# One place in the order of issue for each of 2222 operations, instead of a periodic table of places

## The chip, the cores and the metric

The kernel runs on one core of a Trainium2 chip. The metric is the device time of one execution in microseconds (us). In the profile PE is TensorE's matmul, PEld its weight load, DVE is VectorE, ACT is ScalarE, POOL is GpSimd and SP is SyncE, which here issues DMAs only. An instruction of an engine waits at the head of that engine's queue until what it needs is there, and everything behind it in the same queue waits with it.

## What is computed

Two state-space convolutions (S4D) of the same input, mixed by a gate. The input `u` has 2048 positions and 512 channels; each of the two branches has its own parameters and 128 states for each channel.

```python
def branch(u, log_A_real, A_imag, C_real, C_imag, log_dt, D_skip):
    dt = exp(log_dt)
    A = -exp(log_A_real) + 1j * A_imag
    C = (C_real + 1j * C_imag) * dt[:, None]
    P = exp((A * dt[:, None])[:, :, None] * arange(L))      # channel, state, position
    K = 2.0 * einsum("dn,dnl->dl", C, P).real               # the filter of each channel
    y = irfft(rfft(u.T, 2 * L) * rfft(K, 2 * L))[..., :L]   # causal convolution
    return y.T + u * D_skip
g = sigmoid((u * gate_w).sum(-1, keepdims=True))
out = g * branch_A(u) + (1 - g) * branch_B(u)
```

## The kernel before

All work is float32, apart from the phases, whose angles are carried as three bfloat16 terms. There are 1024 filters (512 channels, two branches). They are worked on in three nested sizes:

- A **chunk** `c` (8 of them) is 128 filters. Its preparation, `prep_ops(c)`, is a list of 34 steps on `[128, 128]` tiles: angles and amplitudes on DVE and ACT (L175 to L198, L256), a split of the angles into three bfloat16 terms (`split`, L216, and `rest`, L221), a bounce of these through device memory by SP (`bounce`, L225, then `back`, L231 and L233, which writes the tile `rot`), and the decay rates by PE and ACT (`turned`, L242 to L244, `dec`, L248). Then `make_bases` (L301) makes 28 exponentials on ACT in seven parts of four, and `amplitudes` (L305) finishes them on DVE.
- A **unit** `u` (64 of them, eight for a chunk) is 16 filters. It has fifteen operations: `phase` on PE (L335, reads `rot`), `sine` (L343), `absf` (L346) and `cosine` (L350) on ACT, two grids (L355) and four products (L371, L383, L389, L393) on DVE, `modes` on PE (64 small matmuls, L401), `keep` on ACT (L408), `skip` on DVE (L413), `s1_k` on PE (L419) and `keep_x` on ACT (L426), which writes a part of the tile `xall`.
- A **block** `b` (16 of them) is four units. Its operations multiply the spectra of the filters with that of the input: `s2` on PE (L463), `products` on DVE (L476), eight of each; four DMAs by POOL, `add_products` (L510), which add one half of the products onto the other half within `xall`; four `inverse` on PE (L521) that wait for these DMAs; four `keep_z` on ACT (L527). The input's own spectrum comes from `s1_u` on PE (L439) and `keep_u` on ACT (L447), and for every second block `keep_v`, `turn_v`, `negate_v` and `both_v` (L487 to L503) lay it out in the tile `v` with ACT and SP's DMAs.

At the end of each quarter of the channels `final` (L548, PE), `final_keep` (L557, ACT) and `final_out` (L560, SP) make the output; the last quarter has a form of its own (L569 to L594). A gate (L602 to L620) is made once near the start. Sin, Exp and Sigmoid need different tables on ACT, which the compiler loads before an ACTIVATE that needs another table than the last one (ACT_TABLE_LOAD in the profile).

What sets the order: every operation is put into a list with a number, its key, and the list is issued in the order of the keys. While it is issued, each instruction of PE, DVE and ACT is tied to the instruction before it on its engine, so the three engines run exactly in this order. A key is a home plus an offset from the table `AT`. One unit is 1.0 of key. The offsets are periodic: a unit's operations have four offsets (by `u % 4`), a block's have one set for even and one for odd blocks, a chunk's 34 steps have one set for all chunks but the first two:

```python
    def op(name, home, fn, i=None, *args):
        at = AT[name] if i is None else AT[name][i]
        ops.append((home + at, len(ops), name, fn, args, (name, i), home))
```

The home of unit `u` is `u`, of chunk `c` it is `8 * (c - 1)`, of block `b` it is `4 * (b + 1)`. So the offset 5.5876 of the last `split` of a chunk and the offset -1.3428 of a chunk's first `phase` place these two 8 - 1.3428 - 5.5876 = 1.07 units apart, in each chunk from the third on. The loops at the end of the function (`for c in range(nchunk)` and those after it) only fill the list. Bounds that the order meets: `rot` has two buffers (by `c % 2`), the tiles of a unit (`f0`, `f1`, `fsn`) two each, `ph`, `pk`, `ps1` and `ks` one each, and the PSUM tiles of `s2`, `s1_u`, `inverse` and `turned` share three.

Of the kernel before, what the change touches and what calls it, by code (L numbers as in the profile page):

```python
# [10 lines left out]
F32 = mybir.dt.float32  # L11
# [29 lines left out]

# [4 lines left out]
def tile_gated_s4d(ctx: ExitStack, tc: tile.TileContext, nsb, a, out):  # L46
    nc = tc.nc
# [57 lines left out]
    for i, (o, x) in enumerate(consts):  # L105
        op("ld", 0, lambda o=o, x=x: nc.sync.dma_start(out=o, in_=x), i)
# [432 lines left out]
    def final(sb, j, dp, r4):  # L539
# [5 lines left out]
        for n in range(2):  # L545
            for rq in range(4):
# [16 lines left out]
    ends_e = []  # L563

    def last_e(g):
        if g % 2 == 0:
            tag = "fsn" if g < 4 else "f0"
            ends_e.append(work.tile([128, 2, 8, 2, 64], F32, name="el", tag=tag, bufs=BUFS[tag]))
            nc.gpsimd.memset(ends_e[-1], 0.0)  # L569
# [64 lines left out]
    d0, p0 = make_dt(), prep_ops(0)  # L634
    for n, fn in enumerate(first + d0 + p0):
        op("first", 0, fn, n)
    for c in range(nchunk):
        h = 8 * (c - 1)
        if c > 0:
            e = AT["early"] if c == 1 else 0  # L640
            op("pl", h if c > 1 else -1, load_pars, None, c)
            op("al", h if c > 1 else -1, decay_rate, None, c)
            for i, fn in enumerate(prep_ops(c)):
                op("prep", h - e, fn, i)
        for i in range(7):
            op("ex", h if c else h + 0.2, make_bases, i, c, i)
        op("ba", h if c else h + 0.2, amplitudes, None, c)
    for u in range(nunit):
        for name, fn in (
            ("ph", phase), ("sn", sine), ("ab", absf),  # L650
            ("cs", cosine), ("g1", grid1), ("g0", grid0), ("p1", prod1), ("pm", prod_minus),
            ("pc", prod_cos), ("pn", prod_sin), ("mo", modes), ("ke", keep), ("kd", skip), ("s1", s1_k), ("xk", keep_x),
        ):
            op(name, u + AT["start"].get((u, name), 0) + AT["stop"].get((nunit - u, name), 0), fn, u % 4, u)
    for b in range(-1, nblk):
        h = 4 * (b + 1)
        if b == 0:
            op("ul0", 0, load_u, None, 0)
        if b >= 1:
# [174 lines left out]
```

## Time and profile before

| | us |
|---|---|
| median of 3 runs | 615.21 |
| lowest and highest run | 611.93 and 618.03 |
| the profiled execution | 612.52 |
| its span, first to last instruction | 610.8 |

The page of the profile gives busy times and shares of each engine, then the span in 40 slices, the DMA queues, the chain of work that ended last and the costliest groups of instructions. Other views give the waits (who waited for whom, in total, how many times, the longest), the chain or the instructions in order of time, and the busy time of each engine in chosen stretches. A few lines of the page beside those shown in the prediction:

```profile
## 4 chain that ended last, share of the span: by engine, by line
PE 33%; ACT 23%; DMA 19%; DVE 16%; issue 5%; SPq 2%; POOL 1%; DVEq 0%; ACTq 0%
DMA xall<-xall 9%; PE psi L521 7%; ACT bas L301 6%; DMA rot<-dsp 6%; PE pk L401 5%; PE ph L335 5%; PE ps L463 4%; PE ps L419 4%; PE pf L548 4%; DMA dsp<-sp 3%; DVE xall L476 3%; DVE f L355 3%; DVE f L383 3%; ACT fsn L343 3%; ACT fsn L346 3%
```

The chain that ended last runs over all engines and the DMAs; its largest single items are `add_products` (`xall<-xall`), `inverse` (`psi`) and the way back of the angles (`rot<-dsp`).

### The profile page before, as it was taken

The page shows a single profiled execution, that of the slowest core. Times are in us where ns is not written, and L with a number is a line of the kernel's source. Part 1 is how long each engine was busy: PE and PEld are TensorE (multiplying, and loading weights), DVE is VectorE, ACT ScalarE, POOL GpSimd, SP SyncE. Part 2 cuts the span into 40 slices and gives each one's busy share as a digit, 9 for nine tenths or more (in the row PEclk, how much of TensorE's full clock was granted, in tenths as well). Part 3 has the DMA queues.
Part 4 walks back from the last instruction along what each step waited for, and adds up shares of the span by engine and source line. Part 5 has one row for each costly group of instructions (what it writes and reads, how often), then busy time and mean ns, then how long its engine had stood idle before and what let it go on. Part 6 is the DMA issues. An engine that isn't in the chain of part 4 may idle for free.

```text
span 610.8 us, 23306 instructions
## 1 busy us (share of the span) xinstructions
PE 498.6 (82%) x10397; PEld 419.0 (69%) x10397; DVE 486.9 (80%) x812; ACT 443.9 (73%) x877; POOL 64.5 (11%) x73
## 2 busy tenths in 40 slices
PE   5879578969598979998598978999598979978756
PEld 3537476858476858877476866878377857867656
DVE  7379599978599986898699795898699885888730
ACT  3589887768589877789588785789588886765611
POOL 2000020021002020021102020020202020020620
PEclk9679878979698987999698897999699997999879
DMA  8852650081604561083604452063603650072441
GB/s 281 263 202 57 109 113 20 5 137 25 132 3 61 98 129 38 30 127 68 119 3 71 88 104 63 29 109 70 119 2 50 110 108 25 29 115 44 71 70 71
DMA packets 95411, 51.39 MB, mean 84 GB/s; under 512 B 79296, under 2 KB 83904, under 8 KB 95312
## 3 DMA queue, kind: packets, MB, share of 16 engines
q1 hardware_dynamic: 90192, 33.13, 23.3%
q0 software_dynamic: 5120, 16.78, 16.4%
q8 instruction: 81, 1.33, 0.9%
q14 instruction: 18, 0.15, 0.1%
HBM read 17.91 MB, written 5.77 MB: 39 GB/s over the span
## 4 chain that ended last, share of the span: by engine, by line
PE 33%; ACT 23%; DMA 19%; DVE 16%; issue 5%; SPq 2%; POOL 1%; DVEq 0%; ACTq 0%
DMA xall<-xall 9%; PE psi L521 7%; ACT bas L301 6%; DMA rot<-dsp 6%; PE pk L401 5%; PE ph L335 5%; PE ps L463 4%; PE ps L419 4%; PE pf L548 4%; DMA dsp<-sp 3%; DVE xall L476 3%; DVE f L355 3%; DVE f L383 3%; ACT fsn L343 3%; ACT fsn L346 3%
## 5 line engine op out<-in xcount | busy, mean ns | idle before, releaser
L355 DVE TENSOR_TENSOR f<-bas 128x1024 f32<-128x1024 f32 (+1 forms) x128 | 119.0, 947 | 6.9 <-PE pk L401 3.8
L463 PE MATMUL ps<-xall,gk 128*64 128x64 f32 (+1 forms) x1728 | 114.2, 255 | 7.0 <-DVE xall L476 5.2
L521 PE MATMUL psi<-mi,xall 128*128 128x128 f32 x512 | 86.9, 325 | 34.4 <-DMA xall<-xall 34.3
L463 PEld LDWEIGHTS ps<-xall,gk 128*64 128x64 f32 (+1 forms) x1728 | 103.2, 157 | 15.3 <-DVE xall L476 6.0
L510 POOL DMA_DIRECT2D xall<-xall x64 | 53.4, 1264 | 520.3 <-ACT v L487 150.8
L521 PEld LDWEIGHTS psi<-mi,xall 128*128 128x128 f32 x512 | 75.9, 229 | 42.4 <-issue 40.0
L476 DVE TENSOR_TENSOR xall<-ps,v 128x512 f32<-128x512 f32 x128 | 85.6, 683 | 18.8 <-PE ps L463 9.2
L419 PE MATMUL ps<-w,ks 128*64 128x128 f32 x1024 | 75.0, 292 | 23.2 <-DVE ks L413 16.6
L335 PE MATMUL ph<-cph,rot 49*128 49x512 bf16 x567 | 62.0, 337 | 28.1 <-DMA rot<-dsp 16.9
L419 PEld LDWEIGHTS ps<-w,ks 128*64 128x64 f32 x1024 | 59.2, 145 | 32.2 <-DVE ks L413 17.4
L383 DVE TENSOR_TENSOR f<-f,fsn 128x1024 f32<-128x1024 f32 x64 | 78.1, 1220 | 3.0 <-ACT fsn L350 3.0
L401 PE MATMUL pk<-f,f 128*32 128x64 f32 x4096 | 77.7, 233 | 0.5 <-ACT ks L408 0.5
L371 DVE TENSOR_TENSOR f<-f,fsn 128x1024 f32<-128x1024 f32 x64 | 77.9, 1217 | 0.0
L401 PEld LDWEIGHTS pk<-f,f 128*32 128x32 f32 x4096 | 66.8, 118 | 11.9 <-issue 6.7
L350 ACT ACTIVATE fsn<-fsn 128x1024 f32<-128x1024 f32 x64 | 69.0, 1078 | 0.3
L408 ACT COPY ks<-pk 128x256 f32<-128x256 f32 x64 | 24.3, 379 | 61.4 <-PE pk L401 52.4
L335 PEld LDWEIGHTS <-rot 49*128 49x128 bf16 x567 | 36.0, 100 | 47.0 <-DMA rot<-dsp 20.7
L343 ACT ACTIVATE fsn<-ph 128x1024 f32<-128x1024 f32 x64 | 66.9, 1045 | 0.1
L346 ACT ACTIVATE fsn<-ph 128x1024 f32<-128x1024 f32 x64 | 66.4, 1038 | 0.0
L527 ACT COPY z<-psi 128x512 f32<-128x512 f32 x64 | 37.7, 605 | 33.2 <-PE psi L521 33.2
L301 ACT ACTIVATE bas<-dec 128x128 f32<-128x128 f32 x224 | 59.5, 485 | 0.1
L389 DVE TENSOR_TENSOR f<-f,fsn 128x512 f32<-128x512 f32 x64 | 43.8, 685 | 11.4 <-ACT fsn L350 11.4
(107 smaller groups left out, 515.9 us busy)
## 6 DMA issues: line engine op xcount, KB each, us to landing
xall<-xall POOLq DMA_DIRECT2D x64, 256.0 KB, 6.6
v<-v SPq DMA_DIRECT2D x64, 128.0 KB, 4.8
uraw<-in_us SPq DMA_DIRECT2D x16, 256.0 KB, 3.6
z<-in_ut SPq DMA_DIRECT2D x16, 256.0 KB, 5.2
out_dram<-ot SPq DMA_DIRECT2D x24, 128.0 KB, 2.1
par<-in_par SPq DMA_DIRECT2D x8, 256.0 KB, 3.5
gk<-in_gk SPq DMA_DIRECT2D x4, 512.0 KB, 6.1
eg<-in_eg SPq DMA_DIRECT2D x4, 512.0 KB, 6.1
```

The source lines that it names most:

```text
L301: S.activation(bases[c][:, :, j], decays[c][:, 0], AF.Exp, scale=-float(s) if s else 0.0)
L335: PE.matmul(o, lt, rh, start=w == 0 and n < 2, stop=w == 2, skip_group_check=True)
L343: S.activation(fsn(u)[:, 1], phs[u], AF.Sin, scale=TWO_PI)
L346: S.activation(fsn(u)[:, 0], phs[u], AF.Abs)
L355: V.tensor_tensor(o.rearrange("p k (a b) -> p k a b", b=8), bas[:, :, hi : hi + n].unsqueeze(3).to_broadcast([128, 16, n, 8]), bas[:, :, l ...
L371: V.tensor_tensor(f1s[u].rearrange("p v k m -> p v (k m)"), f1s[u][:, 1].rearrange("p k m -> p (k m)").unsqueeze(1).to_broadcast([128, 2, ...
L383: V.tensor_tensor(f0[:, :, :, 0:32], f0[:, 1, :, 0:32].unsqueeze(1).to_broadcast([128, 2, 16, 32]), back, OP.mult)
L401: PE.matmul(pk[32 * kd : 32 * kd + 32, i, :], f1[:, p, 4 * i + kd, :], f0[:, p, 4 * i + kd, :], start=p == 1, stop=p == 0, tile_position=( ...
L419: PE.matmul(ps[64 * ri : 64 * ri + 64, i, :], kss[u][:, i, :], w1[:, ri, :], start=True, stop=True, tile_position=(0, 64 * ri),)
L463: PE.matmul(ps[h : h + w, j, 0:n], gk[:, k, h : h + w], xall[:, x0:x1, 2 * k : 2 * k + 2], start=True, stop=True, tile_position=(0, h),)
L476: V.tensor_tensor(k.rearrange("p x (k t) -> p k x t", t=2), p2s[b, g][:, :, 0:64].unsqueeze(2).to_broadcast([128, 4, 2, 64]), v[:, 4 * g : ...
L521: PE.matmul(ps[:, i, :], xk(b)[:, x : x + 2, :].rearrange("p x k -> p (x k)"), mi, start=True, stop=True)
```

## The change

No operation is added, removed or altered. The table `AT` now holds, for every name, one whole number for each operation of that name, in the order in which the loops create them: its place from 0 to 2221 among all operations. The list is issued in the order of these places. So the pattern no longer repeats from chunk to chunk, and any operation can stand anywhere. 44 of the 2222 operations keep their place; the mean shift is 20 places. The table `ends_e` of the last quarter becomes a dictionary, since its four tiles are no longer made in the order of their numbers.

The core of the diff, with the rows of the new table that the prediction reads. The 34 numbers of a chunk in `prep` follow its list of steps; `prep` starts with chunk 1. The last `split` is the 27th, `bounce` and `back` are the 28th and 29th. In `pr` each block has eight numbers, in `iv` four; `ph`, `ke` and `kd` have one for each unit.

```diff
+AT = {
...
+    "ex": [127, 110, 140, 134, 125, 122, 115, 338, 320, 333, 379, 343, 330, 326, 591, 541, 550, 583, 561, 579, 558,
+        800, 777, 811, 787, 783, 791, 806, 1097, 1085, 1113, 1120, 1108, 1091, 1101, 1352, 1312, 1338, 1318, 1331,
+        1344, 1325, 1640, 1630, 1644, 1660, 1653, 1663, 1650, 1872, 1853, 1879, 1876, 1867, 1862, 1883],
...
+    "prep": [95, 101, 107, 109, 104, 106, 112, 114, 102, 99, 116, 103, 118, 111, 105, 113, 119, 120, 121, 144, 152,
+        154, 160, 163, 169, 178, 181, 186, 223, 151, 150, 124, 153, 171, 184, 189, 191, 193, 194, 196, 198, 253,
+        199, 187, 351, 206, 352, 209, 210, 216, 353, 354, 362, 410, 416, 455, 462, 501, 507, 512, 516, 520, 554,
...
+    "ph": [98, 182, 204, 226, 250, 266, 283, 297, 359, 373, 407, 427, 451, 472, 496, 523, 607, 621, 637, 664, 693,
...
+    "ke": [203, 240, 265, 282, 298, 332, 360, 386, 409, 437, 464, 499, 518, 563, 614, 633, 650, 690, 729, 747, 766,
...
+    "kd": [207, 242, 273, 285, 305, 336, 363, 387, 412, 439, 468, 500, 542, 568, 616, 639, 654, 716, 732, 750, 770,
...
+    "ux": [89, 80, 172, 158, 245, 324, 395, 348, 474, 549, 629, 643, 722, 739, 857, 871, 1024, 1084, 1178, 1159,
...
+    "pr": [339, 308, 334, 311, 315, 313, 337, 325, 425, 420, 440, 456, 469, 448, 443, 422, 571, 553, 576, 590, 581,
+        569, 587, 580, 678, 662, 700, 694, 668, 687, 703, 709, 779, 830, 792, 814, 838, 789, 802, 809, 982, 934,
...
+    "iv": [375, 378, 384, 396, 515, 546, 528, 560, 631, 628, 680, 648, 760, 763, 775, 785, 940, 900, 911, 936,
...
-    def op(name, home, fn, i=None, *args):
-        at = AT[name] if i is None else AT[name][i]
-        ops.append((home + at, len(ops), name, fn, args, (name, i), home))
-
-    def op_at(name, key, fn, *args):
-        ops.append((key, len(ops), name, fn, args, None, key))
+    count = {}
+
+    def op(name, fn, *args):
+        i = count[name] = count.get(name, -1) + 1
+        ops.append((AT[name][i], len(ops), name, fn, args))
...
-    ends_e = []
+    ends_e = {}
...
     for u in range(nunit):
-        for name, fn in (
-            ("ph", phase), ("sn", sine), ("ab", absf),
-            ("cs", cosine), ("g1", grid1), ("g0", grid0), ("p1", prod1), ("pm", prod_minus),
-            ("pc", prod_cos), ("pn", prod_sin), ("mo", modes), ("ke", keep), ("kd", skip), ("s1", s1_k), ("xk", keep_x),
-        ):
-            op(name, u + AT["start"].get((u, name), 0) + AT["stop"].get((nunit - u, name), 0), fn, u % 4, u)
+        for name, fn in stages:
+            op(name, fn, u)
...
-    for key, n, name, fn, args, ref, home in sorted(ops, key=lambda o: o[:2]):
+    for key, n, name, fn, args in sorted(ops, key=lambda o: o[:2]):
```

More of the change, by code (lines that the diff above doesn't have):

```diff
@@ L45, in tile_gated_s4d @@
+AT = {
+    "ld": [7, 6, 2, 15, 93, 40, 5, 23, 3, 8, 71],
+    "first": [11, 36, 9, 10, 12, 13, 18, 14, 19, 16, 21, 17, 24, 22, 25, 27, 29, 30, 31, 32, 41, 42, 43, 38, 48,
[8 rows of a table added]
+    "prep": [95, 101, 107, 109, 104, 106, 112, 114, 102, 99, 116, 103, 118, 111, 105, 113, 119, 120, 121, 144, 152,
[135 rows of a table added]
+}
 @with_exitstack
@@ L104, in tile_gated_s4d @@
     consts += [(gk[:, j : j + 8], a["gk"][:, j : j + 8]) for j in range(0, M, 8)]
-    for i, (o, x) in enumerate(consts):
-        op("ld", 0, lambda o=o, x=x: nc.sync.dma_start(out=o, in_=x), i)
+    for o, x in consts:
+        op("ld", lambda o=o, x=x: nc.sync.dma_start(out=o, in_=x))
     v = const.tile([128, M, 128], F32, name="v")
@@ L633, in tile_gated_s4d @@
     first.append(lambda: S.activation(warm, als[0][:, 0:1], AF.Sin, scale=0.0))
-    d0, p0 = make_dt(), prep_ops(0)
-    for n, fn in enumerate(first + d0 + p0):
-        op("first", 0, fn, n)
+    for fn in first + make_dt() + prep_ops(0):
+        op("first", fn)
     for c in range(nchunk):
-        h = 8 * (c - 1)
         if c > 0:
[L640 to L644, printed above, removed]
-        for i in range(7):
-            op("ex", h if c else h + 0.2, make_bases, i, c, i)
-        op("ba", h if c else h + 0.2, amplitudes, None, c)
@@ L648, in tile_gated_s4d @@
[L648 to L660 removed]
+            op("pl", load_pars, c)
@@ new lines, in tile_gated_s4d @@
+            op("al", decay_rate, c)
+            for fn in prep_ops(c):
+                op("prep", fn)
+        for i in range(7):
+            op("ex", make_bases, c, i)
+        op("ba", amplitudes, c)
+    stages = [
+        ("ph", phase), ("sn", sine), ("ab", absf), ("cs", cosine), ("g1", grid1), ("g0", grid0), ("p1", prod1),
+        ("pm", prod_minus), ("pc", prod_cos), ("pn", prod_sin), ("mo", modes), ("ke", keep), ("kd", skip),
+        ("s1", s1_k), ("xk", keep_x),
+    ]
+    for u in range(nunit):
+        for name, fn in stages:
+            op(name, fn, u)
@@ L661, in tile_gated_s4d @@
+    for b in range(-1, nblk):
+        turns = b % 2 and b < nblk - 1
         if b >= 0:
+            op("ul", load_u, b)
             for i in range(2):
-                op("us", 8 * (b // 2) - 8, s1_u, 2 * (b % 2) + i, b, i)
-                op("ux", 8 * (b // 2) - 8, keep_u, 2 * (b % 2) + i, b, i)
+                op("us", s1_u, b, i)
+                op("ux", keep_u, b, i)
         for g in range(8):
-            p = 8 * (b % 2) + g
-            op("s2", h, s2, p, b, g)
+            op("s2", s2, b, g)
@@ L668, in tile_gated_s4d @@
             if b >= 0:
-                op("pr", h, products, p, b, g)
-            if b % 2 and b < nblk - 1:
-                op("kv", h, keep_v, g, b, g)
+                op("pr", products, b, g)
+            if turns:
+                op("kv", keep_v, b, g)
         for i in range(2):
-            if b % 2 and b < nblk - 1:
-                op("vd", h, turn_v, i, b, i)
-                op("vn", h, negate_v, i, b, i)
-                op("ve", h, both_v, i, b, i)
-        for i in range(4):
-            if b >= 0:
-                op("ya", h, add_products, 4 * (b % 2) + i, b, i)
@@ L680, in tile_gated_s4d @@
-        for g in range(4):
-            if b >= 0:
-                op("iv", h, inverse, 4 * (b % 2) + g, b, g)
-                op("iz", h, keep_z, 4 * (b % 2) + g, b, g)
+            if turns:
+                op("vd", turn_v, b, i)
+                op("vn", negate_v, b, i)
+                op("ve", both_v, b, i)
+        if b >= 0:
+            for i in range(4):
+                op("ya", add_products, b, i)
+            for g in range(4):
+                op("iv", inverse, b, g)
+                op("iz", keep_z, b, g)
@@ L684, in tile_gated_s4d @@
     for sb in range(nsb - 1):
-        h = 16 * (sb + 1) + AT["fs"][0]
         for j in range(4):
-            hj = h + 8 * j * AT["fs"][1]
-            for i in range(8):
-                op_at("fs", hj + i * AT["fs"][1], final, sb, j, i // 4, i % 4)
             for dp in range(2):
-                op("fk", hj + (4 * dp + 3) * AT["fs"][1], final_keep, None, sb, j, dp)
-                op("fo", hj + (4 * dp + 3) * AT["fs"][1], final_out, None, sb, j, dp)
+                for r4 in range(4):
+                    op("fs", final, sb, j, dp, r4)
```

39 lines of the change are left out of this document (18 added, 21 removed), and 131 rows, old and new, of the table AT.

## The prediction

> **What bounds the kernel now.** I read the busy times first, then busy time by stage, then the waits of DVE and PE, then the chain through one chunk boundary.
>
> ```profile
> span 610.8 us, 23306 instructions
> PE 498.6 (82%) x10397; PEld 419.0 (69%) x10397; DVE 486.9 (80%) x812; ACT 443.9 (73%) x877; POOL 64.5 (11%) x73
> ...
> 0.00:45.00 45.00, 30.73 (x299) 19.54 (x301) 26.89 (x88) 26.25 (x63) 3.71 (x5) 0.81 0.77 253
> 45.00:147.70 102.70, 82.53 (x1677) 71.39 (x1674) 90.75 (x143) 83.03 (x154) 6.79 (x8) 0.88 0.37 68
> 147.70:561.00 413.30, 352.60 (x7719) 297.39 (x7716) 347.15 (x550) 318.82 (x635) 39.95 (x48) 0.91 0.39 72
> 561.00:610.80 49.80, 32.73 (x722) 30.64 (x720) 22.08 (x34) 15.76 (x28) 14.07 (x12) 0.86 0.31 65
> 156.50:167.50 11.00, 6.72 (x86) 5.12 (x87) 5.21 (x11) 4.17 (x8) 0.00 (x0) 0.53 0.53 104
> 167.50:178.50 11.00, 10.21 (x214) 8.67 (x213) 10.97 (x14) 10.14 (x16) 0.00 (x0) 1.00 0.01 3
> 217.90:288.10 70.20, 63.78 (x1512) 53.72 (x1508) 58.01 (x96) 55.42 (x114) 5.97 (x8) 0.93 0.42 81
> ```
>
> The later rows are busy time by stretch: its length, then PE, PEld, DVE, ACT, POOL, the granted TensorE clock, DMA share, GB/s. No engine is full. DVE idles 45 - 26.89 = 18.1 us in the head, 12.0 in the next stretch, 66.2 in the six chunks from 147.7 to 561 (11.0 in each of 68.9) and 27.7 in the tail. DVE and PE are close: in the chunk of the last row PE works 63.78 of 70.20 us. The two rows of 11 us are a boundary between chunks and what follows: PE idle and half clock first, then DVE full at full clock. Order is what is at stake, since the work fits. The waits, in total, times, and the longest:
>
> ```profile
> DVE ks L413 <- ACT ks L408: 35.6, 17, 5.9
> DVE f L389 <- ACT fsn L350: 11.4, 12, 3.2
> DVE tb L195 <- ACT tb L182: 10.1, 2, 5.4
> DVE xall L476 <- DMA v<-v: 8.3, 2, 6.5
> ...
> PE psi L521 <- DMA xall<-xall: 34.3, 15, 7.4
> PE ph L335 <- DMA rot<-dsp: 16.9, 7, 3.4
> ...
> ACT ks L408 <- PE pk L401: 52.4, 34, 7.1
> ...
> SPq L231 <- DMA dsp<-sp: 18.9, 7, 4.0
> ```
>
> **What the waits come from.** The chain through the boundary before unit 16 (start, length, what), and the DVE row in which it ends:
>
> ```profile
> 144.71 1.28 ACT L301
> 145.99 0.01 issue
> 146.00 4.95 ACT bas L301 x19
> 150.95 0.23 issue
> 151.18 0.45 ACT sp L216
> ...
> 151.64 4.18 DMA dsp<-sp
> ...
> 158.88 4.51 DMA rot<-dsp
> ...
> 163.44 1.46 PE ph L335 x6
> 164.89 1.91 PE pk L401 x64
> ...
> 166.82 0.38 ACT ks L408
> ...
> 167.23 0.17 DVE L413 TENSOR_TENSOR ks<-ks,dl 128x4 f32<-128x4 f32 x1 [5.76 <-ACT ks L408]
> ```
>
> The last split of the angles stands behind the chunk's exponentials on ACT; from it to the first phase that reads `rot` pass 163.44 - 151.18 = 12.3 us. PE waits there, `modes` of an earlier unit waits behind the phase, ACT behind `modes`, and DVE stands 5.76 us at `skip`. So the 35.6 us of DVE are mostly PE's waits for DMAs, passed on.
>
> **The change, part by part.** No work is added except table loads, so each step is a question of cover: how much stands between a producer and its consumer. I count places; one is worth 610.8 / 2222 = 0.275 us on average.
>
> *The way of the angles.* Before, the last split and the chunk's first `phase` are 1.07 units apart, 31 to 38 places in chunks 2 to 7, or 8.5 to 10.5 us for a way of 12.3. In the new table chunk 2 has 516 and 607, and chunks 2 to 7 have 91, 58, 113, 92, 172 and 87 places: 16 us at least, mostly 24 to 47. These PE waits should go. With the split SP's `bounce` and `back` move forward too. `back` holds SP for the bounce's landing (18.9 us in 7 waits, at most 4.0), and behind it in the new table stand for instance an output and a `turn_v` of block 9 (chunk 6: `back` at 1524, these at 1534 and 1543). From `negate_v` to the first product that reads its half of `v` there are now 37 to 125 places, against 34 to 96, so 4 us there stay covered.
> What DVE gets back: the two waits of 10.1 are boundaries (chunks 4 and 6), and four of the 17 at `skip`, by the one shown about 5.6 each, 22.4. That is 32.5, 5.4 a chunk. PE in the chunk shown has only 70.20 - 63.78 = 6.4 us idle, so I take 4.5 back for each: 6 x 4.5 = 27 us.
>
> *The adding DMAs and `inverse`.* One row of the DMA issues and three of PE in order of time:
>
> ```profile
> xall<-xall POOLq DMA_DIRECT2D x64, 256.0 KB, 6.6
> ...
> 130.81 1.41 PE L521 MATMUL psi<-mi,xall 128*128 128x128 f32 x5 [3.66 <-DMA xall<-xall]
> ...
> 569.86 3.64 PE L521 MATMUL psi<-mi,xall 128*128 128x128 f32 x16 [2.55 <-DMA xall<-xall]
> ...
> 591.91 6.31 PE L521 MATMUL psi<-mi,xall 128*128 128x128 f32 x32 [7.38 <-DMA xall<-xall]
> ```
>
> Before, 28 to 41 places lie between a block's last product and its first `inverse` (blocks 0 to 13), and PE still waits (3.66 us in block 1, with 33). Landing alone takes 6.6 us, so some 9 are needed. Now they are 36 to 71 (block 3: 709 to 760, 51 where it had 33), or 10 to 20 us. Of 34.3 us, 7.4 are the last block, which has nothing to put in between (5 places, now 11). The other 26.9 largely go on PE; what of it reached DVE outside the boundaries I put at 1 us a chunk, about half of the 11.4 that DVE waits for `cosine`: 6 us.
>
> *The first turn of `v`.* Products of block 0 wait 6.5 us for it; the places from `negate_v` rise from 34 to 48, some 3.9 us. I take 4.
>
> *Head.* Two rows, of ACT and of DVE:
>
> ```profile
> 21.96 0.58 ACT L447 COPY xall<-ps1u 128x512 f32<-128x512 f32 x1 [5.99 <-PE ps1u L439]
> ...
> 28.84 0.69 DVE L305 TENSOR_TENSOR bas<-bas,dec 128x512 f32<-128x512 f32 x1 [8.41 <-ACT bas L301]
> ```
>
> ACT idles 5.99 us for `s1_u`, behind the long first phase on PE, and the first exponentials stand behind that. Now `keep_u` has places 89 and 80, ahead of the first phase at 98, and the exponentials begin at 110. I take 6 of DVE's 8.41. If the weights of `s1_u` arrive late, `turned` waits behind it: the range reaches to 0.
>
> *Tail.* The last `modes` now stands ahead of block 14's `inverse` instead of behind three of them, so the 2.55 us leave the path, and three `inverse` of block 14 fall into the last wait, which the path has in any case. I take 3; the bounds are 0 and 5.
>
> *What it costs.* Sin and Exp now alternate more. Counted along ACT's order, the table changes rise by 4: the exponentials of chunks 1 and 2 are spread among sines.
>
> ```profile
> L343 ACT ACT_TABLE_LOAD x8 | 10.3, 1283 | 0.1
> ...
> L301 ACT ACT_TABLE_LOAD x7 | 9.0, 1283 | 0.1
> ```
>
> 4 x 1.283 = 5.1 us on ACT, which idles more than that: 1 us on the path. Taken at the full row, it would be 5. The Trainium skill, "ScalarE: Activation LUTs", section "What ACT_TABLE_LOAD costs", speaks against the change more strongly: a switch of sets costs about 2.66 us with its drain. By that the four would be 10.6 us. The trace differs: the next Exp starts 0.01 us after the load's 1.28.
>
> More costly is the hand-over from `keep` to `skip`. In 49 units they are now within five places of each other, against 8 before, so DVE has next to nothing between. Where ACT is late, DVE stands. Outside the boundaries 13 such waits cost 35.6 - 22.4 = 13.2, 1.0 each. Of the 41 more units I let a fifth pay: 8 us. The bounds are 0 and all of them.
>
> *The clock.* At the boundary the granted clock was 0.53, and 64 small matmuls took 1.91 us; in the row after it was 1.00. The Trainium skill, "TensorE: Matmul & The Clock Gate", Part 1, says that an idle window of about 3.4 us halves TensorE's clock and a busy one restores it. The rows agree. By that rule PE would win time beside its waits, at most half of a boundary's 6.72 busy us: 6 x 3.4 = 20 us of PE work, and the mid chunks could give back all 5.4, which makes the sum 5 us better.
>
> **The sum**, against the profiled execution of 612.5 (span 610.8): -27 - 6 - 4 - 6 - 3 + 1 + 8 = -37, so 575.5. The median of the runs, 615.2, is 2.7 above that execution. I put the forecast between: 577.
>
> **The rivals.**
> 1. *The waits move on* (faster, by half). PE is nearly as full as DVE, so what is freed at the boundary meets PE's own queue: half of 33 in the chunks, 3 in the head, 0 in the tail, 2 for `v`, and 9 lost: 612.5 - 12.5 = 600; without the hand-over cost 592. I say 595. For it: 63.78 of 70.20. Against: part of that PE time is half clock.
> 2. *All of it comes back.* DVE idles 12 in the head, 6 and 24 (4 a chunk) in the middle and 22 in the tail: 486.9 + 64 + 1.7 = 553; with 1 + 8 of costs, 562.
> 3. *The change doesn't cover the DMAs.* The angles' transfers and the adds now run among others, and if these lengthen by what the cover gained, 27 + 6 don't come: 612.5 - 13 + 9 = 608.5. Against: DMA share is 0.39 in the middle, and the new distances exceed the need by 4 us and more.
> 4. *Slower: `skip` stalls DVE in every unit.* ACT waits for `modes` 52.4 us in 34 waits, 1.54 each. If each of the 41 tight units passes that on to DVE, 63 us come in where I have 8: 612.5 - 45 + 1 + 63 = 631. It decides from about 45 / 41 = 1.1 us a unit on. Against: from `modes` to `keep` ACT now has more to do in between (the units with under 1 us of it fall from 25 to 7), so ACT itself should be late less often.
>
> **How the numbers follow.** Likeliest, 577 (567 to 588): 0.50. Rival 1: 0.23. Rival 2: 0.13. Rival 3: 0.07. Rival 4: 0.07. About 1% is what a measurement of this kernel can tell from no change. The first three cases are faster by more: 0.86. Rival 3 is within 1%: 0.07. Rival 4: 0.07 slower. The range 560 to 600 holds the first two and most of rival 2, and leaves out rivals 3 and 4 and the ends.
>
> **What would show it.** Right: PE's waits for `rot` in the steady chunks gone and those for `xall<-xall` down to about 8 to 12 us, nearly all in the last blocks; DVE's wait for `ks` under 20; the mean granted clock over 0.91; 23 table loads. Wrong: DVE's wait for `ks` at 60 or more (rival 4); adds landing later than 9 us (rival 3); PE over 95% busy in the middle with DVE idle as before (rival 1).

## The result: 582.4 us

| | median of 4 runs | lowest to highest | profiled execution | its span | mean granted clock |
|---|---|---|---|---|---|
| before | 613.57 us | 609.87 to 618.03 | 612.52 us | 610.8 us | 0.897 |
| after | 582.41 us | 577.19 to 586.56 | 582.86 us | 581.1 us | 0.924 |

The ratio is 0.9461, with a 95% interval of 0.9356 to 0.9565: 5.4% faster. The forecast was 577, with a range of 560 to 600. Three of the four times of before are those given further up. The medians are over all runs; the ratios, here and below, leave out every run that took over 1.5% longer than the fastest of its kernel. All lines of the code are 145 higher in the new kernel, because its table is longer: the line that waits in `skip` was L413 and is L558.

The page's busy line of the kernel after, and below it the busy time by stretch (length, PE, PEld, DVE, ACT, POOL, granted clock, DMA share, GB/s). The middle stretch is now 382.3 us long, where it was 413.3.

```profile
PE 488.6 (84%) x10397; PEld 410.0 (71%) x10397; DVE 497.6 (86%) x812; ACT 453.5 (78%) x882; POOL 64.2 (11%) x73
```

```profile
0.00:45.00 45.00, 35.49 (x338) 21.05 (x339) 29.44 (x94) 28.62 (x69) 3.71 (x5) 0.92 0.75 248
45.00:147.70 102.70, 83.01 (x1738) 70.19 (x1736) 98.57 (x148) 94.97 (x175) 6.92 (x8) 0.88 0.42 78
147.70:530.00 382.30, 335.06 (x7585) 286.05 (x7575) 347.10 (x539) 316.52 (x616) 39.93 (x48) 0.94 0.41 76
530.00:581.00 51.00, 35.01 (x763) 32.73 (x758) 22.46 (x34) 13.37 (x25) 13.68 (x12) 0.87 0.31 64
```

DVE does 347.1 us of work in the middle, as before, but idles 382.3 - 347.1 = 35.2 us there instead of 66.2. In the two rows ahead of it DVE idles 15.6 and 4.1 us instead of 18.1 and 12.0, in the tail 28.5 instead of 27.7. In all it idles 40.4 us less; its busy time is 10.7 higher (the last section has more on that), which leaves 29.7. How far each kernel had come at a time is told better by the start of some blocks' last product, read from both traces:

| start of block's last product (us) | 0 | 1 | 2 | 3 | 7 | 11 | 14 | 15 | end of the span |
|---|---|---|---|---|---|---|---|---|---|
| before | 81.4 | 121.3 | 149.6 | 191.7 | 328.5 | 467.8 | 562.5 | 584.8 | 610.8 |
| after | 82.4 | 120.6 | 150.1 | 181.6 | 314.3 | 442.4 | 532.4 | 555.0 | 581.1 |
| ahead by | -1.0 | 0.7 | -0.5 | 10.1 | 14.2 | 25.4 | 30.1 | 29.8 | 29.7 |

Up to 150 us no block is clearly sooner. Differences of a few us say little there: in the kernel after and the six runs below that issue the same operations up to this point, block 0's number lies between 81.7 and 85.6. DVE has done more by then (the durations of the instructions that start before 147.7 us add up to 141.1 us, before to 133.8), but what it did is work for later blocks. From there to 532 us the lead grows to 30 us, and from the last product on the two kernels take 26.0 and 26.1 us.

The waits of the kernel after, first those of DVE, then of PE, then one of ACT (in total, times, longest):

```profile
...
DVE f L534 <- ACT fsn L495: 9.7, 6, 6.5
...
DVE ks L558 <- ACT ks L553: 7.2, 5, 2.7
```

```profile
PE ph L480 <- ACT fsn L488: 15.0, 15, 2.8
PE ps L564 <- DVE ks L558: 14.7, 12, 4.7
...
PE psi L666 <- DMA xall<-xall: 4.7, 2, 4.4
```

```profile
ACT ks L553 <- PE pk L546: 7.5, 7, 3.1
```

DVE's wait in `skip` fell from 35.6 to 7.2 us, ACT's wait for `modes` from 52.4 to 7.5, PE's wait for the adding DMAs from 34.3 to 4.7. PE's wait for `rot` fell from 16.9 to a single one of 1.4 (row below). Those of DVE for `tb` (10.1) and for `v` (8.3) are no longer among the large ones. What is left on PE is spread over many short waits for ACT's sines and DVE's `skip`.

One boundary still stands, that of chunk 3, whose first unit is 24. PE in order of time, with its idle time and what ended it in brackets:

```profile
220.14 0.58 PE L480 MATMUL ph<-cph,rot 49*128 49x512 bf16 x1 [4.85 <-issue]
222.08 1.46 PE L480 MATMUL ph<-cph,rot 49*128 49x256 bf16 x8 [1.35 <-DMA rot<-dsp]
```

"Issue" says that the profile shows no releaser. Here 58 places lie between the last `split` and the first phase, the fewest of the six chunks, and PE idles 4.85 and 1.35 us. DVE's longest wait for the cosine, the 6.5 in the list above, is the one behind this phase.

### The profile page after: what moved, and what is told of

It is laid out like the page before. It is cut to its first block, busy times and chain, and to the rows that moved or that the text cites. A ratio compares the mean times of both kernels' runs of the same rounds, so it can differ in the third digit from the quotient of the medians.

```text
span 581.1 us, 23321 instructions
## 1 busy us (share of the span) xinstructions
PE 488.6 (84%) x10397; PEld 410.0 (71%) x10397; DVE 497.6 (86%) x812; ACT 453.5 (78%) x882; POOL 64.2 (11%) x73
## 5 line engine op out<-in xcount | busy, mean ns | idle before, releaser
L608 PE MATMUL ps<-xall,gk 128*64 128x64 f32 (+1 forms) x1728 | 116.9, 254 | 3.8 <-ACT xall L592 1.0
L546 PE MATMUL pk<-f,f 128*32 128x64 f32 x4096 | 79.1, 233 | 24.8 <-issue 10.8
L564 PE MATMUL ps<-w,ks 128*64 128x128 f32 x1024 | 76.4, 296 | 18.7 <-DVE ks L558 14.7
L621 DVE TENSOR_TENSOR xall<-ps,v 128x512 f32<-128x512 f32 x128 | 83.4, 683 | 9.1 <-ACT fsn L488 4.4
L491 ACT ACTIVATE fsn<-ph 128x1024 f32<-128x1024 f32 x64 | 66.6, 1040 | 29.7 <-PE ph L480 18.8
L666 PE MATMUL psi<-mi,xall 128*128 128x128 f32 x512 | 76.7, 303 | 5.2 <-DMA xall<-xall 4.7
L564 PEld LDWEIGHTS ps<-w,ks 128*64 128x64 f32 x1024 | 60.8, 147 | 27.9 <-DVE ks L558 15.2
L480 PE MATMUL ph<-cph,rot 49*128 49x512 bf16 x567 | 60.7, 341 | 21.3 <-ACT fsn L488 15.0
L666 PEld LDWEIGHTS psi<-mi,xall 128*128 128x128 f32 x512 | 67.8, 210 | 12.4 <-issue 9.5
L446 ACT ACTIVATE bas<-dec 128x128 f32<-128x128 f32 x224 | 64.1, 489 | 0.1
L480 PEld LDWEIGHTS <-rot 49*128 49x128 bf16 x567 | 35.9, 101 | 36.3 <-issue 24.7
L672 ACT COPY z<-psi 128x512 f32<-128x512 f32 x64 | 38.0, 606 | 19.6 <-PE psi L666 19.4
L571 ACT COPY xall<-ps 128x512 f32<-128x512 f32 x64 | 38.6, 604 | 12.8 <-PE ps L564 12.7
```

The lines of the kernel that those rows point to most:

```text
L480: PE.matmul(o, lt, rh, start=w == 0 and n < 2, stop=w == 2, skip_group_check=True)
L491: S.activation(fsn(u)[:, 0], phs[u], AF.Abs)
L546: PE.matmul(pk[32 * kd : 32 * kd + 32, i, :], f1[:, p, 4 * i + kd, :], f0[:, p, 4 * i + kd, :], start=p == 1, stop=p == 0, tile_position=( ...
L564: PE.matmul(ps[64 * ri : 64 * ri + 64, i, :], kss[u][:, i, :], w1[:, ri, :], start=True, stop=True, tile_position=(0, 64 * ri),)
L608: PE.matmul(ps[h : h + w, j, 0:n], gk[:, k, h : h + w], xall[:, x0:x1, 2 * k : 2 * k + 2], start=True, stop=True, tile_position=(0, h),)
L621: V.tensor_tensor(k.rearrange("p x (k t) -> p k x t", t=2), p2s[b, g][:, :, 0:64].unsqueeze(2).to_broadcast([128, 4, 2, 64]), v[:, 4 * g : ...
```

## The experiments

The time of each against runs of the kernel before that were measured beside it, as a ratio with its 95% interval. One per cent is 6.1 us. The medians of those runs of before lie between 610.1 and 613.6 us, so two rows are better compared by their ratios than by their medians.

| run | what it is | median, us | ratio | interval |
|---|---|---|---|---|
| after | the change | 582.41 | 0.9461 | 0.9356 to 0.9565 |
| u_rot | after, angles' way short again, harshly | 615.65 | 1.0073 | 1.0035 to 1.0112 |
| u_rot_eq | after, angles' way shortened more mildly | 586.10 | 0.9567 | 0.9489 to 0.9646 |
| u_inv | after, adds' cover short again | 601.70 | 0.9819 | 0.9753 to 0.9885 |
| u_both_eq | u_rot_eq and u_inv together | 601.64 | 0.9834 | 0.9762 to 0.9905 |
| u_head | after, first 300 operations in the old order | 580.82 | 0.9494 | 0.9442 to 0.9546 |
| u_tail | after, last 162 operations in the old order | 581.31 | 0.9533 | 0.9469 to 0.9597 |
| d_rot | before, angles' way 60 places longer | 601.16 | 0.9815 | 0.9740 to 0.9890 |
| d_both | before, both covers longer | 608.90 | 0.9895 | 0.9779 to 1.0012 |
| b_tight | before, each `skip` directly behind its `keep` | 620.87 | 1.0139 | 1.0037 to 1.0242 |
| a_head | after, one load moved | 577.79 | 0.9383 | 0.9296 to 0.9469 |
| a_ch3 | after, chunk 3's way longer | 575.84 | 0.9395 | 0.9317 to 0.9472 |
| a_three | both of these and an edit in the tail | 563.84 | 0.9196 | 0.9116 to 0.9277 |

In the diffs only places change. Other operations keep their relative order and move up or down by the few places that this leaves.

### The angles' way undone: u_rot and u_rot_eq

The places of the last `split`, `bounce` and `back` of chunk 2 (first phase at about 607) and of chunk 6 (1676), in `prep`; u_rot first, then u_rot_eq, each against the kernel after. The `theta`, `t1` and `t0` of the next chunk and one load of `par` move behind them.

```diff
-  ... 507, 512, 516, 520, 554, ... 1497, 1501, 1504, 1507, 1524, ...
+  ... 507, 512, 571, 589, 605, ... 1497, 1501, 1640, 1658, 1674, ...
```

```diff
-  ... 507, 512, 516, 520, 554, ... 1497, 1501, 1504, 1507, 1524, ...
+  ... 507, 512, 559, 577, 593, ... 1497, 1501, 1634, 1652, 1668, ...
```

> The changed order, with one part undone: the last split of the angles, its bounce and its way back stand again 31 to 38 places ahead of the first phase of chunks 2 to 7, as before, instead of 58 to 172 (where the next chunk's first three steps on the same tiles stood in between, they move behind). Theory A (the gain is in the boundaries between chunks: PE waited for the angles and DVE behind it): PE waits for rot in five or six boundaries again, some 15 us, DVE's wait for ks rises from 7.2 to 25 or more, and 20 to 27 of the 31 us are lost: 602 to 610 us. Rival B (the gain comes from the order as a whole, and each single wait is replaced by another): PE waits again but less than 10 us are lost: under 592 us.

> The kernel after, with the way of the angles (last split, bounce, way back) of chunks 2 to 7 put so that TensorE reaches the chunk's first phase about 7 to 9 us after the split, as it did in the kernel before, instead of the 4 to 8 us of the harsher undo. Theory (the boundaries carry most of the gain, and what is lost goes with what TensorE still has to do): TensorE's waits for rot come back at about 17 us in 6 or 7 stalls of some 3 us, as before, the DVE waits for fsn behind them grow to about 20 us, and 12 to 22 of the 31 us are lost: 594 to 604 us. Rival (the stalls are paid only in part, the new order around them takes them up): under 588 us. Rival (any shift of these steps costs as the harsher undo did): 610 us or more.

A wait of PE in u_rot, then the same in u_rot_eq:

```profile
PE ph L480 <- DMA rot<-dsp: 37.3, 7, 8.4
```

```profile
PE ph L480 <- DMA rot<-dsp: 9.6, 4, 5.5
```

u_rot loses all of the gain: 33 us by the medians, 37 by the ratios, more than either case expected. But it is harsher than the kernel before was. From `split` to phase it has 33 to 40 places, the kernel before 31 to 38, and yet PE gets to the phase 4.3 to 8.0 us after the end of the split, where before it got there after 7.1 to 9.0 (at five of the six boundaries it had stood 0.8 to 3.0 us for the adds on the way). Its waits for `rot` are 37.3 us, more than twice the 16.9 of before. So here about one us is lost for each us that PE waits for the angles.

u_rot_eq errs to the other side. PE gets to the phases 6.5 to 10.2 us after the split, about as before, but the angles are sooner there: the last part of `rot` lands 7.0 to 10.1 us after the split (14.0 in chunk 3), where before it took 10.8 to 12.2. Of its 9.6 us of waits 6.1 are those of chunk 3, which the kernel after has too (4.85 and 1.35), so only 3.5 are new. The ratio rises by 0.0106, some 6 us, with intervals that overlap, and the span of the profiled execution, 580.4 us, is no longer than the 581.1 of the kernel after. So the price of this wait goes with how late the angles are when PE comes for them, not with the number of places, and u_rot_eq doesn't bring the waits of the kernel before back: it can't price them. At one us for one, the 16.9 us of before would be worth 17 us at most, an estimate from u_rot.

### The adds' cover undone: u_inv and u_both_eq

The places of `inverse` of blocks 3 and 5, as an example; u_inv does this for blocks 0 to 14, so that 29 to 42 places lie behind a block's last product (18 for block 14), and `keep_z` moves along.

```diff
-  "iv": [... 760, 763, 775, 785, ... 1047, 1100, 1093, 1064, ...
+  "iv": [... 743, 747, 765, 775, ... 1031, 1086, 1080, 1051, ...
```

> The changed order, with another part undone: inverse and keep_z stand again 28 to 41 places behind their block's last product in blocks 0 to 14 (18 in block 14), as before, instead of 36 to 71. Theory A, as the prediction's sum has it: PE's waits for xall<-xall rise from 4.7 to 25 us or more, of which about 6 reach the end: 586 to 592 us. Rival B: PE has other idle time in the same places and nothing is lost: 579 to 585 us. A third possibility, that these waits were worth as much as the boundaries: 595 us or more.

> The run before this one (the way of the angles as near as it was before) and, on top, the inverses and kept products of blocks 0 to 14 back to 29 to 42 places behind their last product, which alone had cost some 19 us. If the two losses add: 613 to 622 us, the kernel before or slower. If they overlap, because both waits hold up the same boundary in turn: 603 to 610 us, with TensorE waits for xall near 25 us and for rot under 12 us.

One wait of PE and one of DVE in u_inv (in u_both_eq PE's is 28.3 us):

```profile
PE psi L666 <- DMA xall<-xall: 27.6, 11, 7.3
...
DVE ks L558 <- ACT ks L553: 22.8, 11, 4.1
```

This cover is worth 0.9819 - 0.9461 = 3.6%, about 22 us by the ratios and 19 by the medians: two thirds of the gain, where the prediction gave it 6. The way to the end is in the rows. PE stands before `inverse` for 27.6 us instead of 4.7, and the `modes` queued behind it come late, so `keep` on ACT and `skip` on DVE do too: DVE's wait in `skip` rises from 7.2 to 22.8, and that for the cosine from 9.7 to 13.5. Together that is 19.4 us.

With both undone the time is that of u_inv alone, 601.6 us, where 603 to 610 was expected if the losses overlap. This alone doesn't show that they do, since u_rot_eq puts so little of the angles' wait back. One boundary shows it. PE at the first phase of chunk 3 in u_inv, to be set beside the two rows of the kernel after; then the boundary of chunk 2 in the kernel before:

```profile
226.32 2.04 PE L666 MATMUL psi<-mi,xall 128*128 128x128 f32 x8 [4.48 <-DMA xall<-xall]
228.30 1.46 PE L480 MATMUL ph<-cph,rot 49*128 49x512 bf16 x9
```

```profile
158.03 2.05 PE L521 MATMUL psi<-mi,xall 128*128 128x128 f32 x8 [2.63 <-DMA xall<-xall]
162.64 0.60 PE L335 MATMUL ph<-cph,rot 49*128 49x512 bf16 x1 [2.56 <-DMA rot<-dsp]
```

In the kernel after PE idles 4.85 and 1.35 us at this phase. In u_inv it stands 4.48 us for the adds just ahead of it, and then finds the angles there: the first wait hides the second (in u_both_eq too, with 5.51 us for the adds). In the kernel before the two stand in a row between split and phase at five of the six boundaries, so what is lost there can't be given to one of them alone.

u_both_eq keeps 1.7% of the gain. Which of the other moves holds them (the turn of `v` was not undone by itself), and how much of it is the angles' way that isn't really put back, stays open.

### One part alone in the old order: d_rot and d_both

In the order of before, all preparation of chunks 2 to 7 is moved ahead by 60 places; from `split` to phase there are then 83 to 89. As an example the last `split`, `bounce` and `back` of chunk 2, as places in the issued list (the operations that they pass close up behind them). d_both moves `inverse` too, of block 3 for example.

```diff
-  split 564, bounce 579, back 594
+  split 516, bounce 531, back 548
```

```diff
-  "iv": [... 735, 743, 765, 754, ...
+  "iv": [... 761, 769, 790, 776, ...
```

> The old order, with one part of the change alone: every step of the preparation of chunks 2 to 7 (with its load and decay rate) 60 places earlier, so that the last split of the angles stands 83 to 89 places ahead of the first phase that reads them instead of 31 to 38. Theory A (the boundaries carry the gain, and the cover of the angles is enough for it): PE's 16.9 us for rot and DVE's boundary waits go, 16 to 27 us are won: 586 to 597 us. Rival C (at a boundary PE waits for the adds of the block first and for the angles after that, so one wait stands in for the other): under 10 us are won, 603 us or more, with PE's wait for xall<-xall well over 34 us.

> The old order, with both parts: the preparation 60 places earlier, and inverse and keep_z of blocks 0 to 13 as far behind their block's last product as in the changed order (31 to 66 places instead of 28 to 41; outputs that need them move behind them). Theory A: a little more than the angles alone, 580 to 592 us. Rival C: far more than the angles alone, by 10 us or more. Rival B (the whole order is needed): over 600 us.

A wait of PE in d_rot, then waits of PE and DVE in d_both:

```profile
PE psi L666 <- DMA xall<-xall: 42.4, 15, 7.4
```

```profile
PE ps L564 <- DVE ks L558: 27.2, 15, 3.5
...
PE psi L666 <- DMA xall<-xall: 10.7, 2, 7.4
...
DVE xall L621 <- PE ps L608: 35.9, 26, 4.1
```

In d_rot the waits for `rot` are gone, 16.9 us, and 1.9% come in, some 11 us: between the two cases expected. The waits for the adds rise from 34.3 to 42.4 at the same time. Part of that may be freed time that is waited for again one step later. But the moved preparation also takes places away from the adds: in every second block 22 to 28 are left between last product and `inverse`, where there were 28 to 35. No run tells the two apart. In d_both these waits are down to 10.7, yet 1.1% are left, with an interval that reaches to no gain at all; that is the case in which the whole order is needed. DVE now waits 35.9 us for the products of PE (9.2 in the kernel before), and PE 27.2 (16.6) for `skip`. A reading that fits, but was not tested: the `inverse`, put further back, stands in front of other work, and that comes late. So the two covers alone are not the change. They bring what they do in the kernel after only with the units, products and inverses around them set anew.

### The hand-over from `keep` to `skip`: b_tight

The order of before with each `skip` directly behind its `keep`, here units 0 to 3:

```diff
-  keep 172, 198, 237, 262    skip 175, 205, 249, 270
+  keep 172, 198, 237, 262    skip 173, 199, 238, 263
```

> The old order, with each skip directly behind its keep (one place) instead of mostly six to ten behind it. It measures the hand-over that the prediction priced at 8 us for 41 more close pairs. By that price, 0.2 us a pair with 64 pairs: 8 to 13 us slower, 621 to 626 us, with DVE's wait for ks up by about as much. By its slower rival, 1.5 us a pair: 60 us or more slower. By what the changed kernel's trace shows (DVE's wait for ks fell to 7.2 us although 49 of 64 pairs are close): within 4 us, 609 to 617 us.

```profile
DVE ks L558 <- ACT ks L553: 72.6, 30, 7.3
```

DVE's wait at `skip` doubles, from 35.6 to 72.6 us, and the time rises by 1.4%, 8.5 us (2 to 15 by the interval). Most of the new wait replaces waits that DVE had elsewhere: it idles 129.9 us in all, where it idled 123.9. A row of the waits says where an engine stands, not what it costs to stand there. The 8 us that the prediction set for 41 closer pairs are in that range for the old order, where 56 came closer, and 63 us are not. In the kernel after DVE waits only 7.2 us at `skip` with pairs as close; ACT's small wait for `modes`, 7.5 us, fits that.

### Head and tail in the old order: u_head and u_tail

The first 300 and the last 162 operations of the kernel after, each group in the relative order that it had before.

> The changed order, with its first 300 operations in the old table's relative order; everything behind them is the changed order. By the prediction's step (6 us in the head): 586 to 590 us. By the two traces (when 5 to 10% of DVE's work is done, both stand at the same time; in the changed kernel the first decay rates are ready at 19.8 us instead of 12.9, because the identity and the weights stand behind a load that SP waits with): nothing is lost, 579 to 585 us, or a little is won.

> The changed order, with its last 162 operations in the old table's relative order. By the prediction's step (3 us in the tail): 585 to 587 us. By the two traces (the last skip of the changed kernel stands behind four copies of DVE that wait for POOL's memsets, and PE waits 4.7 us for it, which takes back what block 14's moved inverse gave): 580 to 584 us.

Neither can be told from the kernel after: the new order within the head, and within the tail, brings nothing that these runs resolve.

### Where the head's gain went: a_head

One place is changed, that of the load of chunk 1's `par`:

```diff
-  "pl": [1, 117, 278, 539, 842, 1092, 1392],
+  "pl": [23, 117, 278, 539, 842, 1092, 1392],
```

> The kernel after, with one load alone moved: chunk 1's par load goes behind the loads of ident and w on SP's queue, where it had stood ahead of them and waited for the single par buffer. If SP's standing there is what ate the head's gain: ident lands near 2.7 us instead of 8.3, the first turned tile of chunk 0 comes 4 to 7 us sooner, and the time is 575 to 578 us. If the head is bound otherwise (table loads and the first angles on ACT): the early tiles come sooner, the first ks does not, and the time stays within 2 us of 582.

SP's queue, PE, ACT and DVE in the head of the kernel after (start, length, what, and in brackets the idle time ahead of it with its releaser), then the matching rows of a_head:

```profile
4.02 0.43 SPq L251 DMA_DIRECT2D ph<-in_ph  x1
8.67 0.34 SPq L221 DMA_DIRECT2D par<-in_par  x1
9.05 0.43 SPq L251 DMA_DIRECT2D ident<-in_ident  x1
10.01 0.43 SPq L251 DMA_DIRECT2D w<-in_w  x1
...
11.69 0.40 ACT L382 ACTIVATE dg<-ident,dt 128x128 f32<-128x128 f32 x1 [5.36 <-DMA ident<-in_ident]
...
15.48 3.41 PE L584 MATMUL ps1u<-w,uraw 128*64 128x128 f32 x32 [3.57 <-DMA w<-in_w]
18.83 0.49 PE L387 MATMUL pt<-ident,al 128*128 128x128 f32 x2
...
24.84 0.68 DVE L450 TENSOR_TENSOR bas<-bas,dec 128x512 f32<-128x512 f32 x1
```

```profile
4.49 0.42 SPq L251 DMA_DIRECT2D ident<-in_ident  x1
5.44 0.43 SPq L251 DMA_DIRECT2D w<-in_w  x1
8.69 0.33 SPq L221 DMA_DIRECT2D par<-in_par  x1
...
11.62 0.40 ACT L382 ACTIVATE dg<-ident,dt 128x128 f32<-128x128 f32 x1 [4.97 <-DVE tb L343]
...
11.10 1.97 PE L584 MATMUL ps1u<-w,uraw 128*64 128x128 f32 x32
13.00 0.49 PE L387 MATMUL pt<-ident,al 128*128 128x128 f32 x2
...
20.51 0.68 DVE L450 TENSOR_TENSOR bas<-bas,dec 128x512 f32<-128x512 f32 x1
```

There is one `par` buffer, so the second load of it can't be issued before chunk 0's parameters have been read; SP's wait ends with `theta` on DVE (`tb`). In the kernel after this load stands ahead of `ident` and `w`, and SP issues in order: from 4.45 to 8.67 us it issues nothing. The load that counts is that of `w`, the weights of `s1_u`. PE stands 3.57 us for it, and chunk 0's `turned` (`pt`), which stands behind `s1_u`, starts at 18.83 us instead of 13.00. ACT's wait of 5.36 us, put down to `ident`, is no loss of its own: in a_head `dg` starts only 0.07 us sooner, since it then waits for DVE (`ident` lands at 9.3 us instead of 11.7, not at 2.7 as expected).

The first use of the exponentials on DVE is at 24.84 us. With the load behind them it is at 20.51, against 28.84 in the kernel before. So 4.3 us come in at that point; at the last product of block 0 it is 3.0 us (79.4 against 82.4), at block 1's 2.8. In a_three below, with the same edit, these are 1.5 and 1.9; both runs are ahead of all seven that share the old place of the load. By the ratios a_head is 0.8% better, with intervals that overlap: the traces show the gain at the first blocks, and the times allow it. (The profiled execution took 581.2 us, 3.4 above the median of its runs, so its later part isn't compared.)

### The one boundary that was left: a_ch3

Chunk 3's last remainder step, its last `split`, `bounce` and `back`; from `split` to phase are now 104 places instead of 58.

```diff
-  ... 674, 688, 771, 818, 821, 845, ...
+  ... 674, 688, 736, 772, 775, 800, ...
```

> The kernel after, with chunk 3's way of the angles alone made longer, from 58 places to 104 (its last remainder step, split, bounce and way back go earlier). If the stall at chunk 3's first phase (TensorE idle some 1.4 and 4.9 us there, DVE 6.5 us behind it) is a loss of its own: gone, and 574 to 578 us. If it is made up by the next wait: 580 to 583 us.

PE at the same phase in a_ch3, and DVE's wait for the cosine, to be set beside the two rows of chunk 3 and the 9.7 us above:

```profile
215.38 0.83 PE L480 MATMUL ph<-cph,rot 49*128 49x512 bf16 x9
```

```profile
DVE f L534 <- ACT fsn L495: 3.4, 5, 1.5
```

The stall is gone, the cosine's wait falls from 9.7 to 3.4, and the last product of block 5 starts at 244.0 instead of 251.8. The lead stays to the end: block 14 is 6.6 us sooner (525.8 against 532.4), the span 6.8 (574.3 against 581.1). By these traces a boundary of the angles' way is worth 6 to 7 us here, where PE idled 6.2 us and no adds stand in front of it; by the ratios a_ch3 is 0.7% better, 4 us, with intervals that overlap.

### A version that beats both: a_three

The two edits above, and one in the tail, where four copies of `last_e_copy` on DVE stand ahead of the last `skip` and are held up by memsets on POOL. The last `keep` and `skip` go ahead of them (last numbers of `ke` and `kd`, whole row of `le2`):

```diff
-  "ke": [... 2161]    "kd": [... 2162]    "le2": [2166, 2195, 2159, 2160, 2170, 2173, 2153, 2157]
+  "ke": [... 2157]    "kd": [... 2158]    "le2": [2166, 2195, 2161, 2162, 2170, 2173, 2159, 2160]
```

> The changed order with three edits of it. Head: the load of chunk 1's parameters, with which SP waits for a buffer, moves behind the loads of the identity and the weights. Chunk 3: last split, bounce and way back 45 places earlier (this chunk had the least distance, 58 places, and PE still waits 6.2 us there). Tail: the last skip moves ahead of four copies of DVE that wait for POOL. If these are local losses that the traces show rightly: 4 to 6 us in the head, 4 to 6 in chunk 3, 3 to 4 in the tail, 567 to 573 us. If what is won at one place is waited for again at the next: 577 to 583 us, with the first unit's modes earlier than 42 us all the same.

DVE, POOL and PE in the tail of the kernel after, and PE's row at the same work in a_three:

```profile
535.94 8.11 POOL L714 MEMSET el<- 128x2048 f32 x4
...
540.60 4.75 DVE L719 COPY el<-eg 64x512 f32<-64x512 f32 x4 [0.89 <-POOL el L714]
545.38 0.17 DVE L558 TENSOR_TENSOR ks<-ks,dl 128x4 f32<-128x4 f32 x1
...
545.60 1.98 PE L564 MATMUL ps<-w,ks 128*64 128x128 f32 x16 [4.74 <-DVE ks L558]
```

```profile
537.53 1.09 PE L564 MATMUL ps<-w,ks 128*64 128x128 f32 x16 [1.39 <-DVE ks L558]
```

The copies hold DVE from 540.60 to 545.35, and the last unit's `skip`, 0.17 us long, stands behind them with PE waiting 4.74 us. The first copy alone takes 3.74 us, where the others take 0.42: it ends 0.29 us after the last memset (544.05). In a_three the first copy takes 2.11 and ends 0.28 us after the last memset, but `skip` is ahead of it, and PE's wait is 1.39. (The trace of a_three is of an execution of 572.4 us, the longest of its four.)

The ratio, 0.9196, lies with its whole interval below that of the kernel after: 2.6%, some 16 us better, and the median, 563.8, is below the 567 to 573 expected if all three are losses of their own. By the ratios a_head has 0.8% of it and a_ch3 0.7%. The rest, 1.2%, would be the tail's, but that edit was not run alone, and each of these shares is uncertain by about as much as it is large. The traces say the same of the tail: from the start of block 14's last product to the end a_three takes 42.9 us, against 48.7 in the kernel after and 48.5 in a_ch3, which has the same tail as the kernel after.

## Why the prediction was right, and where its steps were off

The case held likeliest is the one that came: the waits of a boundary go, DVE gets most of them back, and the price is small. Its marks: the waits for `rot` are gone but for 1.4 us in chunk 3, `skip` is at 7.2 us, the clock at 0.924, and the waits for the adds fell to 4.7, below the 8 to 12 foreseen. The sum was -37, and -29.7 came between the two profiled executions; the forecast of 577 was 5 us low. That the sum fits is in part luck: shares within it were off by more, and in both directions:

- *Boundaries, the angles' way: 27 us.* Too much for this step alone. PE's waits for the angles were 16.9 us in all, one us of them costs about one (u_rot), and without them the old order gains 11 (d_rot). The step that failed is the assignment: the whole wait in `skip` behind a boundary was put to the angles, since their wait is the last on PE. At five of the six boundaries PE stands for the adds ahead of it, and u_inv shows at chunk 3 that this wait can hide the one for the angles. Where no adds stand in front (chunk 3 in the kernel after), a boundary of the angles is worth 6 to 7 us.
- *The adding DMAs: 6 us.* Too little. u_inv measured 19 to 22. The prediction counted only what reached DVE outside the boundaries, and gave the adds' part of the boundaries to the angles. The two together, 33 in the prediction, have about the right size: 30 us of lead come in between 150 and 532 us.
- *First turn of `v`: 4.* The wait is gone, but block 0's last product starts at 82.4 us instead of 81.4, a difference within what equal heads show (81.7 to 85.6). DVE has done other work in that time; whether it pays later was not tested.
- *Head: 6.* It didn't come. The first exponentials are used 4.0 us sooner, but the blocks up to 150 us are no sooner, and u_head gives the same time as the kernel after. The prediction named the condition (weights of `s1_u` that arrive late, with `turned` behind them) and did not read SP's queue to see that it would come: `par` for chunk 1 in place 1 stops SP for 4.2 us, PE waits 3.57 us for `w`, and a_head and a_three get 1.5 to 3 us back at block 0.
- *Tail: 3.* None came. The order of `inverse` and `modes` did what was said, but the copies on DVE, put ahead of the last `skip`, cost PE 4.74 us. That the moved copies are held up by POOL was not followed.
- *Hand-over: a cost of 8.* b_tight gives 8.5 in the old order, with 2 to 15 by its interval. In the kernel after it can't be seen by itself.
- *Table loads: 23 foreseen, 24 came, a cost of 1 on the path.* The count was of changes between Exp and Sin alone. The rows below show what it missed.
- *Not in the sum: DVE's own order.* DVE is 10.7 us longer busy with the same instructions. The last section says where that comes from.

Rival 1, the waits moving on, did not decide, and its mark is missing: PE is busy for 335.06 of 382.30 us in the middle, 88% and not over 95. But d_both shows that its mechanism is real: with both covers alone, in the old order, waits for products and for `skip` take their place. Rival 3 falls with the wait of 4.7 for the adds, rival 4 with `skip` at 7.2. Rival 2, 562, took it that DVE would idle 64 us in all, 24 of them in the middle and 22 in the tail, with the same busy time; it idles 83.5, 35.2 in the middle and 28.5 in the tail, and is busy longer.

One bound was wrong. The prediction held every new distance to exceed the need by 4 us and more. Places were turned into time by their mean over the kernel; in chunk 3 PE was through its 58 places 7.8 us after the split, the last part of the angles landed after 14.6 us (10.8 to 12.2 in the kernel before), and the stall stayed.

Three readings of the prediction are off without a bearing on the sum. The two waits of DVE for `tb` (232.7 and 372.7 us) stand at the boundaries of chunks 3 and 5, not 4 and 6. Rival 4 counts the 1 us of table loads twice: its gains without that are 46, and its time is 630.5. And that the rows agree with the rule cited there for TensorE's clock holds for the two clocks, 0.5 and 1.0, but not for the length of the idle window: the granted clock falls to 0.5 at 156.84 us, and no idle time of PE in the ten us before it is longer than 2.66.

## What to carry to other kernels

Where two waits follow each other on one engine, the first can hide the second, and the last wait on the path doesn't say whose the loss is: undo or remove each alone, and both, before the gain is given to one of them. Look in the trace of an undone part whether its wait is really back, before its time is used. A distance in the order of issue is no time: read, in the trace, how long the engine that will wait takes from the issue to the use, and how long the transfer takes. When operations are moved, follow each queue that they enter for one that waits for something there (a load for its single buffer, a copy for a memset), because everything behind it waits too. And look at what stands directly behind what on DVE: an instruction that reads its neighbour's result starts later than one that doesn't.

## What the runs showed of the chip beyond that

ACT in the head of the kernel after, around chunk 1's arctangent:

```profile
25.50 3.96 ACT L446 ACTIVATE bas<-dec 128x128 f32<-128x128 f32 x16
29.48 1.28 ACT L331 ACT_TABLE_LOAD   x1
30.77 0.31 ACT L331 ACTIVATE rc<-rc 128x128 f32<-128x128 f32 x1
31.10 1.28 ACT L332 ACT_TABLE_LOAD   x1
32.40 0.31 ACT L332 ACTIVATE axy<-rc 128x128 f32<-128x128 f32 x1
```

The arctangent behind an exponential takes a load of its own, and the sine right behind it another. For chunk 0, where a sine had run before (its load starts at 4.53 us), the arctangent at 12.08 and the sine at 12.42 needed none. So the set that is loaded for an arctangent alone doesn't serve the sine that follows, and where these operations stand decides over two loads instead of one. The Trainium skill, "ScalarE: Activation LUTs", section "What ACT_TABLE_LOAD costs", puts a switch at 1283 ns and a drain of some 1380 ns. The load agrees, 1.28 us. No drain is seen on either side of it: the load starts 0.02 us after the exponentials end (29.46), and the arctangent 0.01 us after the load.

DVE's busy time rose from 486.9 to 497.6 us with the same 812 instructions. Their own durations add up to 544.0 and 546.3, so longer instructions are the smaller part. The records of neighbours overlap less, 57.2 and 48.7 us in all. Three rows of DVE in the kernel after show what decides it: a grid of `f1`, the product that reads this grid, and products of a block, which read neither.

```profile
177.95 0.68 DVE L500 TENSOR_TENSOR f<-bas 128x512 f32<-128x512 f32 x1
178.66 1.23 DVE L516 TENSOR_TENSOR f<-f,fsn 128x1024 f32<-128x1024 f32 x1
179.81 1.28 DVE L621 TENSOR_TENSOR xall<-ps,v 128x512 f32<-128x512 f32 x2
```

The product starts 0.03 us after the end of the grid that it reads; the next row starts 0.08 us before the product's end. In the whole trace 158 instructions are released by the DVE instruction directly ahead of them, and they start 0.03 to 0.11 us after its end; in the kernel before there are 41. Most of the others overlap with their neighbour, by 0.08 us in the median. In b_tight and d_both, whose order is built on the old one, there are 41 and 37, so it isn't the waits for other engines. By the rows 117 more such neighbours, at 0.11 us or more each, are some 13 us of DVE's time, an estimate. What they cost in the end no run shows. It is one reason why the gain, 29.7 us in the span, is smaller than the fall in DVE's idle time (123.9 to 83.5).
